# A convolution and expert-layer kernel: a new order for its first transfers, tap matrices and tap matmuls

## The chip, the cores and the metric

The kernel runs on one core of a Trainium2 chip. The metric is the device time of one execution in microseconds (us). Of 52 executions of the kernel before, 47 lie within 0.25% (692.39 to 694.08 us) and five reach up to 696.3, so medians over several runs are given, and for the small effect of this study the traces count for more than the times. The **head** is the stretch from the start to the first product with w_out; a **landing** is the end of a transfer.

## The reference, cut to what matters

```python
# x: (8, 4096, 192), weight: (8 heads, 7 taps); w_in: (192, 2048), w_out: (2048, 192)
w = softmax(weight, axis=-1)
out[b, s, head] = sum_k w[head, k] * x_padded[b, s + k, head]     # 7 taps, causal
h = out.reshape(32768, 192) @ w_in
result = np.maximum(0.01 * h, h) @ w_out                          # float32
```

## The kernel before: the parts that the change touches

The rows are handled in groups; the first 18 are half-blocks of 256 positions of two sequences. A group has 8 **units**: 12 matmuls with w_in into one of two output buffers (`ph`, in PSUM), then one activation on ScalarE into `g`. Products with w_out (`po`) follow one group behind. In the main loop VectorE makes the convolution. For the first two half-blocks ("half 0", "half 1") part of it is done by TensorE: a tap is a diagonal 64x64 matrix, in a high and a low bf16 part, and the 7 taps of a chunk of 64 channels are 28 small **tap matmuls** into `acc`, which ScalarE then scales into `yt`.

```python
# pieces of w_in: units 0-1, units 2-3, units 4-7
pieces = (0, NFC // 4, NFC // 2, NFC)
...
load_w_in(0, 0); ...; load_w_in(0, 1)
load_first(1)                      # half 1's x, two transfers
for n in (1, 2):
    for e in range(2):
        load_w_in(n, e)
load_first(2)                      # half 2's x
... # w_out in one transfer, then the x of half 3 and of block 2
diag_wide(0, 0, K)                 # VectorE: chunk 0, high part, all taps at once
for e in range(2):
    cast_first(0, e, nc.scalar.copy)
diag_low(0, range(2))              # ScalarE: low part, one tap each
transpose_first(0)
warm(3)                            # dummy matmuls
...
evac_first(0, nc.vector.tensor_copy, nc.scalar.copy)
...
diag_low(0, range(2, K))
diag_wide(1, 0, K)                 # VectorE: chunk 1, high part
diag_low(1, range(K))
...
for c in range(NPEC):              # half 0's chunks 0 and 1
    pe_jobs, evac_y = pe_conv_jobs(groups[0], c)
    for job in pe_jobs:
        job()
    evac_y(act_scale)              # the scaling, on ScalarE
    if c == 0:
        warm(2)
... # group 0, unit by unit:
mm1(grp, u)
if i == 0 and u == 1:
    transpose_first(1)
    evac_first(1, nc.vector.tensor_copy, nc.vector.tensor_copy)
    ...
if i == 0 and u in (2, 5):         # half 1's taps: 14 behind unit 2, 14 behind unit 5
    n = len(pe_ahead) // 2
    for job in pe_ahead[(u - 2) // 3 * n : (u + 1) // 3 * n]:
        job()
if i == 0 and u == 5:
    evac_y(act_scale)
if i == 0 and u == 6:
    transpose_first(2)
```

## Time and profile before

| | before |
|---|---|
| median of the first 3 runs | 693.94 us (693.4 to 695.55) |
| span of the profiled run | 690.8 us |
| TensorE busy | 685.0 us, 99% |
| TensorE's idle time | 2.3 us, all before 22 us |

What is added here is TensorE's timeline from 16 to 23 us (start, length, engine, line, operation, output and inputs, partitions and elements, count, and in brackets the idle time before it and what ended it):

```profile
16.37 1.50 PE L402 MATMUL ph<-yt,w_in 64*128 64x256 bf16 x23 [0.69 <-DMA w_in<-in_moe_w_in_dram]
17.80 0.96 PE L212 MATMUL acc<-xt,diag 64*64 64x256 bf16 x14
18.69 0.84 PE L402 MATMUL ph<-yt,w_in 64*128 64x256 bf16 x12
...
21.74 0.85 PE L402 MATMUL ph<-yt,w_in 64*128 64x256 bf16 x12 [0.24 <-ACT g L409]
22.39 0.82 PE L428 MATMUL po<-w_out,g 64*128 64x192 bf16 x15
```

Unit 4 resumes at 16.37, when the last piece of w_in has landed. Then come unit 5, half 1's second 14 taps, unit 6 at 18.69. At 22.39 the products with w_out begin; from there to the end of the span the view of waits lists none of TensorE. This is a good point to measure by: the **distance** from unit 4's resumption to the first product is 22.39 - 16.37 = 6.02 us.

### The profile page before, as it was taken

Reading aid. Unit: us, or ns where it says so; the run is one execution under the profiler, and the core shown is the slowest. Engines: PE = TensorE matmul, PEld = TensorE weight load, DVE = VectorE, ACT = ScalarE, POOL = GpSimd, SP = SyncE. Lnnn points to the kernel's source line nnn. Section 1 sums busy time; section 2 is a strip of 40 time slices with the busy share of each in tenths; the row PEclk is TensorE's granted clock in tenths of the full one; section 3 lists DMA queues with packets and bytes.
Section 4 is the critical chain, followed back from the end, with each engine's and each line's share of the span. In section 5 each row is a group of like instructions: output and inputs, shape, how many; then the busy total and the mean of one; then the engine's idle time right before and its main releaser. Section 6 shows DMA issues by size and latency. Waiting matters only on the chain.

```text
span 690.8 us, 26984 instructions
## 1 busy us (share of the span) xinstructions
PE 685.0 (99%) x12190; PEld 600.9 (87%) x12190; DVE 550.4 (80%) x1051; ACT 527.0 (76%) x609; POOL 147.2 (21%) x206
## 2 busy tenths in 40 slices
PE   8999999999999999999999999999999999999998
PEld 6999999999988888888888888888888888888887
DVE  6999999999986787878787878877878878787812
ACT  6888888888898777777777777777777777777771
POOL 7822220222222202222202222102222112000000
PEclk9999999999999999999999999999999999999999
DMA  9976644556657545566445566445664555222112
GB/s 150 121 92 92 83 72 81 70 74 84 81 75 90 73 80 74 67 94 82 68 83 68 75 83 89 71 74 75 78 82 75 82 71 70 67 60 59 47 42 65
DMA packets 184163, 53.85 MB, mean 78 GB/s; under 512 B 149104, under 2 KB 183664, under 8 KB 184048
## 3 DMA queue, kind: packets, MB, share of 16 engines
q0 software_dynamic: 99536, 14.76, 30.2%
q1 hardware_dynamic: 84512, 37.38, 22.7%
q8 instruction: 95, 1.56, 1.0%
q14 instruction: 20, 0.16, 0.1%
HBM read 29.88 MB, written 25.17 MB: 80 GB/s over the span
## 4 chain that ended last, share of the span: by engine, by line
PE 96%; DMA 1%; ACT 1%; POOL 1%; issue 0%; DVE 0%; POOLq 0%
PE po L428 49%; PE ph L402 47%; DMA w_in<-in_moe_w_in_dram 1%; ACT g L409 1%; POOL w_in L248 0%; POOL x_rows L123 0%; PE acc L212 0%; POOL sel L233 0%; DVE o_sb L475 0%; PE ptr L156 0%; POOL ident masks.py:199 0%; POOL sel L231 0%; POOL ident masks.py:197 0%; PE ptr L149 0%; POOLq masks.py:199 0%
## 5 line engine op out<-in xcount | busy, mean ns | idle before, releaser
L409 ACT ACTIVATE g<-ph 128x1024 bf16<-128x1024 f32 x512 | 496.3, 1021 | 142.3 <-PE ph L402 141.8
L193 DVE SCALAR_TENSOR_TENSOR yt<-xt,wk,yt 128x512 bf16<-128x512 bf16 (+1 forms) x720 | 458.3, 637 | 21.1
L428 PE MATMUL po<-w_out,g 64*128 64x192 bf16 (+1 forms) x8064 | 387.6, 243 | 0.0
L402 PE MATMUL ph<-yt,w_in 64*128 64x512 bf16 (+1 forms) x3936 | 384.6, 329 | 1.7 <-DMA w_in<-in_moe_w_in_dram 0.7
L428 PEld LDWEIGHTS <-g 64*128 64x128 bf16 (+1 forms) x8064 | 360.8, 94 | 28.3 <-issue 0.2
L402 PEld LDWEIGHTS <-w_in 64*128 64x128 bf16 x3936 | 246.1, 111 | 53.7 <-issue 3.0
L78 POOL DMA_DIRECT2D x_bf<-in_x_dram x180 | 133.9, 776 | 424.9 <-DMA xt<-x_bf 422.3
L475 DVE COPY o_sb<-po 128x192 f32<-128x192 f32 x184 | 65.7, 357 | 109.4 <-PE po L428 100.6
L187 DVE TENSOR_SCALAR yt<-xt,wk 128x512 bf16<-128x512 bf16 (+1 forms) x120 | 41.0, 341 | 1.5 <-DMA xt<-x_bf 1.4
L475 ACT COPY o_sb<-po 128x192 f32<-128x192 f32 x72 | 23.0, 319 | 3.9 <-PE po L428 0.2
L282 PE MATMUL warm<-zero 128*128 128x256 bf16 (+1 forms) x22 | 5.2, 393 | 1.1 <-DVE junk L228 1.1
L212 PE MATMUL acc<-xt,diag 64*64 64x256 bf16 x84 | 5.7, 283 | 0.0
L212 PEld LDWEIGHTS <-diag 64*64 64x64 bf16 x84 | 4.5, 112 | 1.2 <-DVE wk L362 0.4
L127 POOL DMA_DIRECT2D x_half<-in_x_dram x6 | 4.3, 720 | 3.5 <-DMA w_in<-in_moe_w_in_dram 3.5
L168 DVE COPY xt<-ptr 128x384 bf16<-128x384 bf16 x7 | 2.2, 351 | 3.1 <-PE ptr L156 2.7
L282 PEld LDWEIGHTS <-zero 128*128 128x128 bf16 x22 | 2.6, 132 | 2.3 <-DVE junk L228 1.1
L248 POOL DMA_DIRECT2D w_in<-in_moe_w_in_dram x6 | 3.9, 657 | 0.0
L343 ACT ACTIVATE diag<-ident,whm 128x64 bf16<-128x64 bf16 x14 | 3.5, 337 | 0.0
L123 POOL DMA_DIRECT2D x_rows<-in_x_dram x4 | 2.9, 733 | 0.4 <-DMA w_in<-in_moe_w_in_dram 0.4
L368 ACT ACTIVATE yt<-acc,rsum 128x256 bf16<-128x256 f32 x3 | 1.4, 470 | 1.0 <-PE acc L212 1.0
L288 ACT ACT_TABLE_LOAD x1 | 1.3, 1283 | 0.8 <-PEq L576 0.8
L133 ACT CAST x_half<-x_nat 128x384 bf16<-128x384 f32 x2 | 1.0, 512 | 1.1 <-DMA x_nat<-in_x_dram 1.1
(37 smaller groups left out, 12.0 us busy)
## 6 DMA issues: line engine op xcount, KB each, us to landing
out_dram<-o_sb SPq DMA_DIRECT2D x117, 192.0 KB, 2.1
x_bf<-in_x_dram POOLq DMA_DIRECT2D x180, 64.0 KB, 3.3
out_dram<-o_sb SPq DMA_DIRECT2D x22, 96.0 KB, 1.6
xt<-x_bf SPq DMA_TRANSPOSE x90, 2.5
w_in<-in_moe_w_in_dram POOLq DMA_DIRECT2D x4, 192.0 KB, 5.3
w_in<-in_moe_w_in_dram POOLq DMA_DIRECT2D x2, 384.0 KB, 8.6
w_out<-in_moe_w_out_dram POOLq DMA_DIRECT2D x1, 768.0 KB, 11.6
x_nat<-in_x_dram SPq DMA_DIRECT2D x2, 192.0 KB, 2.6
```

What stands on the lines that cost most here:

```text
L78: nc.gpsimd.dma_start(out=t[:, c, :, e, :], in_=src[2 * rp + e, :, :, c * CH : (c + 1) * CH],)
L127: nc.gpsimd.dma_start(out=x_half[q][:, c, :, e, :], in_=rows[:, e, :, c * CH : (c + 1) * CH],)
L187: lambda s=src, d=dst, c=c: nc.vector.tensor_scalar_mul(d, s, wk[:, c, 0:1])
L193: lambda s=src, d=dst, c=c, k=k: nc.vector.scalar_tensor_tensor(out=d, in0=s, scalar=wk[:, c, k : k + 1], in1=d, op0=mybir.AluOpType.mult, ...
L212: lambda k=k, p=p, a=a, e=e, ps=ps: nc.tensor.matmul(out=acc[ps, :T], lhsT=diag[c][ps, p, k, :], rhs=xt[0][ps, c, a : a + T], start=(k == ...
L248: nc.gpsimd.dma_start(out=w_in[n][e * CH : (e + 1) * CH], in_=moe_w_in[:, fs].rearrange("(c p) f -> p c f", p=CH),)
L282: nc.tensor.matmul(out=wa[:, 0, 0:cols], lhsT=zero[:, 0:128], rhs=zero[:, 0:cols], start=True, stop=True,)
L343: nc.scalar.activation(out=diag[c][:, 1, k, :], in_=ident2, func=mybir.ActivationFunctionType.Copy, scale=whm[:, c, 1, k : k + 1],)
L402: nc.tensor.matmul(out=ph[:, e, i * T : (i + 1) * T], lhsT=w_in_of(f, ps, c), rhs=y[ps, c, t0 : t0 + T], start=(c == 0), stop=(c == NCH - 1),)
L409: act = nc.scalar.activation(out=g[blk][:, nf * u : nf * (u + 1), :, t0 : t0 + T], in_=ph.rearrange("p e (i t) -> p i e t", i=nf), func=my ...
L428: return nc.tensor.matmul(out=po[m], lhsT=g[b][ps, fc, e, s * 128 : (s + 1) * 128], rhs=w_out[ps, fc, :], start=start, stop=stop,)
L475: ins = copy(out=o_sb[:, n % 2, :], in_=po.pop(n))
```

## The change

Its intent, as I read it: fill TensorE's wait for the last w_in piece with half 1's taps, so that they don't stand behind it; get the matrices for half 0 ready sooner by giving chunk 0's to VectorE and chunk 1's to ScalarE, without the two dummy matmuls between the chunks; and bring the second w_in quarter in sooner, since half 1's taps now come later.

```diff
-    def pe_conv_jobs(grp, c):
+    def pe_conv_jobs(grp, c, parts=(0, 1)):
...
     load_w_in(0, 1)
+    for e in range(2):
+        load_w_in(1, e)
     load_first(1)
-    for n in (1, 2):
-        for e in range(2):
-            load_w_in(n, e)
+    for e in range(2):
+        load_w_in(2, e)
     load_first(2)
...
-    diag_wide(0, 0, K)
+    for p in range(2):
+        diag_wide(0, p, K)
     for e in range(2):
         cast_first(0, e, nc.scalar.copy)
-    diag_low(0, range(2))
+    diag_each(1, 1, range(4))
...
+    evac_first(0, nc.vector.tensor_copy, nc.scalar.copy)
     nc.vector.reciprocal(rsum, rsum)
-    evac_first(0, nc.vector.tensor_copy, nc.scalar.copy)
...
-    diag_low(0, range(2, K))
-    diag_wide(1, 0, K)
-    diag_low(1, range(K))
+    diag_each(1, 1, range(4, K))
+    diag_each(1, 0, range(K))
...
-        pe_jobs, evac_y = pe_conv_jobs(groups[0], c)
+        pe_jobs, evac_y = pe_conv_jobs(groups[0], c, (c, 1 - c))
...
-        if c == 0:
-            warm(2)
...
-                if i == 0 and u in (2, 5):
-                    n = len(pe_ahead) // 2
-                    for job in pe_ahead[(u - 2) // 3 * n : (u + 1) // 3 * n]:
+                if i == 0 and u == 3:
+                    for job in pe_ahead:
                         job()
-                if i == 0 and u == 5:
                     evac_y(act_scale)
```

More of the change, by code (lines that the diff above doesn't have):

```diff
@@ L205, in pe_conv_jobs @@
         jobs = []
-        for p in range(2):
+        for p in parts:
             for k in range(K):
@@ L214, in pe_conv_jobs @@
                             rhs=xt[0][ps, c, a : a + T],
-                            start=(k == 0 and p == 0), stop=(k == K - 1 and p == 1),
+                            start=(k == 0 and p == parts[0]),
+                            stop=(k == K - 1 and p == parts[1]),
                         )
@@ L339, in diag_wide, with diag_each @@
         )
-    def diag_low(c, ks):
+    def diag_each(c, p, ks):
         for k in ks:
             nc.scalar.activation(
-                out=diag[c][:, 1, k, :], in_=ident2,
-                func=mybir.ActivationFunctionType.Copy, scale=whm[:, c, 1, k : k + 1],
-            )
-    diag_wide(0, 0, K)
+                out=diag[c][:, p, k, :], in_=ident2,
+                func=mybir.ActivationFunctionType.Copy, scale=whm[:, c, p, k : k + 1],
+            )
+    for p in range(2):
+        diag_wide(0, p, K)
     for e in range(2):
         cast_first(0, e, nc.scalar.copy)
-    diag_low(0, range(2))
+    diag_each(1, 1, range(4))
     transpose_first(0)
```

## The prediction

> **What bounds the kernel now.** I read the page first: engine shares and the chain that ended last.
>
> ```profile
> PE 685.0 (99%) x12190; PEld 600.9 (87%) x12190; DVE 550.4 (80%) x1051; ACT 527.0 (76%) x609; POOL 147.2 (21%) x206
> ...
> PE 96%; DMA 1%; ACT 1%; POOL 1%; issue 0%; DVE 0%; POOLq 0%
> ```
>
> The span of 690.8 us is TensorE work for 96% of its chain. The change adds and removes no product of the main loop, so it can only act where TensorE waits. The view of waits, for TensorE alone over the whole span, lists those:
>
> ```profile
> PE warm L282 <- DVE junk L228: 1.1, 1, 1.1
> PE ph L402 <- DMA w_in<-in_moe_w_in_dram: 0.7, 1, 0.7
> PE ph L402 <- ACT yt L368: 0.3, 1, 0.3
> PE ph L402 <- ACT g L409: 0.2, 1, 0.2
> ```
>
> Columns: who waited, for whom, us in total, times, longest. That is all the idle time there is, and all of it lies before 22 us. So the next view is the chain of waits in that stretch, in order of time (start us, length us, what):
>
> ```profile
> 5.26 1.84 POOL w_in L248 x3
> 7.10 9.23 DMA w_in<-in_moe_w_in_dram
> 16.32 0.05 issue
> 16.37 1.50 PE ph L402 x23
> 17.87 0.89 PE acc L212 x14
> 18.75 0.78 PE ph L402 x12
> 19.53 0.31 PE ptr L156 x24
> 19.84 0.80 PE ph L402 x12
> 20.64 0.02 issue
> 20.66 1.03 ACT g L409
> 21.70 0.04 issue
> 21.74 0.85 PE ph L402 x12
> ```
>
> The reader is to see that everything up to 16.32 us on this path is one transfer: the second half of the last w_in piece (units 4 to 7). What TensorE does before 16.37 isn't on the path; it waited 0.69 us there. From 16.37 to 21.74 the path is TensorE, then ScalarE, and holds 14 tap matmuls of half 1 (acc, 0.89). From 21.74 on there is no wait of TensorE left. So the question is only **how early the matmuls of 21.74 start**: the rest of the span, 690.8 - 21.74 = 669.1 us, should follow unchanged.
>
> **What the Trainium skill says.** "TensorE: Matmul & The Clock Gate", section "What's actually happening": TensorE runs at half rate until it has been busy for one window of about 3.4 us, and the window is free-running. The trace agrees: tap matmuls start 211 ns apart up to 7.4 us and 109 ns apart after it. The same section's idle limit of one window isn't approached by the gaps here (0.7 us at most). The same page, "Architectural detail", has ScalarE and VectorE as strict FIFO; so the place of each tap-matrix operation in its engine's order counts, not only what it waits for. "DMA: Bandwidth & Descriptors", "Two DMAs through the same engine are not ordered": within one queue of an engine descriptors start in order. The trace agrees: the landings of the software queue come in order of issue. w_in quarter 0 at 6.80 and 8.53; half 1's x at 9.05 and 9.74; quarter 1 at 10.55 and 12.59; the last piece at 14.48 and 16.32; half 2's x at 16.84 and 17.36. These I get by adding each issue's start to its time to landing in the tile view. "Perfetto Trace Analysis", "Tensor Engine Instruction": matmul ends are estimated by the profiler, so I work with starts.
>
> **The change, part by part.**
>
> 1. *Order of transfers.* Quarter 1 goes ahead of half 1's x, the bytes before the last piece stay the same, and the issues (0.63 to 0.74 us each) end at the same 6.49 us. So the last piece lands at **16.32 as before**. Quarter 1 should land by 12.59 - (9.74 - 8.53) = 11.4, and half 1's x, now last of the group, at about 12.0 and 12.5: half 2's x, which also follows a w_in piece, adds 0.52 us per share, and the group as a whole ends at 12.59.
>
> 2. *Tap matrices and half 0.* The wide VectorE operation (0.62 us) for chunk 1 becomes one for chunk 0's low part, ahead of the small sums. VectorE was idle 0.46 us before its copy of the first transposes, so this fits: the copy stays at 5.92. ScalarE still makes 14 matrices, 238 ns apart, four instead of two ahead of its copy at 5.95; it was idle 0.56 us there, two cost 0.48, so it fits too. Its last matrix then starts at 8.48 rather than 8.95. TensorE: chunk 0's 28 tap matmuls start at 6.56 as before, last pair at 8.40. Two dummy matmuls (warm) go, with their mode switches: chunk 1 starts at 8.51 instead of 8.92. Its 14 pairs at 0.109 end their starts at 9.92 (10.37 before). All matrices are ready in time (the seventh high one ends at 8.82, is used at 9.9). ScalarE's scaling of chunk 1 (0.47) goes from 10.69 to 10.24, and unit 0 resumes at 10.76, not 11.21: **0.45 us earlier, but ahead of a transfer that decides**.
>
> 3. *Half 1's transposes* follow unit 1. TensorE reaches them at about 12.08 (12.53 before), but their x lands at about 12.5: some 0.45 us of new wait, so they start at about 12.57, as before. VectorE's copy of them starts at 12.96 before and about 12.99 after, and the chain of half 1's convolution on VectorE (ready at 20.48 before) doesn't move.
>
> 4. *Half 1's tap matmuls.* Before: 14 behind unit 2, 14 behind unit 5. After: 28 behind unit 3. Units 2 and 3 start at 12.95 and 13.6 and need about 0.65 each; 28 taps from 14.45 need 14 x 0.109 = 1.52, so TensorE is at unit 4 at about 16.1. Still before 16.32; **the wait for the last piece shrinks from 0.69 to about 0.25 us, its end stays at 16.37**.
>
> 5. *After 16.37* 14 tap matmuls (0.89) and the scaling on ScalarE (0.48) are gone. Not all counts. ScalarE's activation takes 1.02 us per unit against 0.65 to 0.8 for TensorE's 12 matmuls, and there are two buffers, so the rows of ScalarE decide (start, length, what, count, idle before):
>
> ```profile
> 17.25 1.94 ACT L409 ACTIVATE g<-ph 128x1024 bf16<-128x1024 f32 x2 [0.61 <-PE ph L402]
> 19.08 0.48 ACT L368 ACTIVATE yt<-acc,rsum 128x256 bf16<-128x256 f32 x1
> 19.57 4.08 ACT L409 ACTIVATE g<-ph 128x1024 bf16<-128x1024 f32 x4
> ```
>
> ScalarE is busy from 17.25 to 23.65 with hardly a gap: taking away the scaling moves it by 0.4 to 0.48. Step by step: units 4 and 5 as before (activations end 18.28 and 19.19). Unit 6 needs unit 4's buffer: starts at 18.32 (18.69), done 19.14; its activation 19.19 to 20.21 (20.60 before). Transposes of half 2, then unit 7 at 19.39, activation 20.25 to 21.27 (21.69). The next group's unit 0 starts at 20.25, with chunk 2 of VectorE ready only at 20.48: a wait of perhaps 0.05 that nobody feels. Its unit 1 needs unit 7's buffer: 21.31, not 21.74.
>
> The sum: **-0.43 us**, from ScalarE's scaling leaving the stretch, and not the sum of what TensorE lost (0.45 + 0.89 + warm). 693.94 - 0.43 = 693.5.
>
> **The rivals.**
>
> *Half 1's x becomes the bound.* If it lands later than 12.6, say 13.1, transposes, units 2 and 3 and 28 taps all shift, TensorE arrives at unit 4 at 16.6 instead of 16.1, and VectorE's chain ends near 21.0, where the next group's unit 0 needs it at 20.5. Then the gain is eaten and up to 0.3 us lost: 693.6 to 694.3. For it: the slack is only 0.25 us on TensorE and nearly none on VectorE. Against: the bytes ahead of x grow by quarter 1 alone, and that group of four transfers ended at 12.59. I give it 0.3.
>
> *ScalarE doesn't bind and the whole 0.89 comes free.* Then unit 1 of the next group would start at 20.85, time 693.05. Against: ScalarE's rows above have no gap to shrink. 0.1.
>
> *Nothing is seen*: VectorE's later groups bind, and give the gain back. VectorE needs about 10.2 us per half-block (three chunks of about 3.3, plus copies) against TensorE's 10.5; it is ready at 31.20 for a group that TensorE starts at 31.77, with the third chunk used 0.2 later. 0.43 us fits, barely; the margin grows by some 0.5 us per group. 0.15.
>
> *Clock phase.* If the clock opens later than 7.4 us in a run, half 0's taps run longer, up to 0.1 us per pair; the remaining slack of about 0.25 us at unit 4 is less than the 0.69 that hid it before.
>
> **Range and chances.** The effect is 0.06%, while three runs of the kernel before span 693.4 to 695.55. So the range is that of run-to-run difference around 693.5: 692.5 to 694.9. 2% would be 13.9 us, six times all idle time of TensorE (2.3 us); slower by 2% would need a new wait in every group. So: faster 0.01, same 0.98, slower 0.01.
>
> **What would show it.** The wait of TensorE for ScalarE's scaling ends near 10.76; a new wait for half 1's x before the transposes, which start near 12.55; 28 taps in one piece from about 14.45; the wait for w_in ends at 16.37 but is about 0.25 long; ScalarE's activations run without scaling between them; the row at 21.74 comes near 21.31; no wait of TensorE after it; span about 690.4. It is wrong if x lands past 12.7, if the last w_in piece lands elsewhere than 16.3, or if TensorE waits on VectorE after 20 us.

## The result, and the profile after

| | before | after |
|---|---|---|
| median | 693.67 us (692.65 to 695.55, 4 runs) | 692.92 us (692.65 to 693.38, 4 runs) |
| span of the profiled run | 690.8 us | 690.9 us |
| ratio | | 0.9987, 95% interval 0.9964 to 1.0009 |

A ratio here compares the runs of both kernels from the same rounds, so it isn't quite the ratio of the medians. The interval holds 1. The profiled spans are the same within 0.1 us, so the first look at the trace shows no gain at all. TensorE's waits after:

```profile
PE ptr L156 <- DMA x_rows<-in_x_dram: 1.3, 2, 1.0
PE warm L284 <- DVE junk L229: 1.1, 1, 1.1
PE ph L403 <- ACT g L410: 0.7, 2, 0.5
PE ph L403 <- ACT yt L371: 0.3, 1, 0.3
PE acc L212 <- ACT xt L168: 0.2, 1, 0.2
```

Against the four lines of before: the wait of a matmul for w_in has left the list, a wait for half 1's x (`x_rows`) of 1.3 us has come, and the wait for ScalarE's activation rose from 0.2 to 0.7. TensorE's timeline from 12 to 23 us:

```profile
12.55 0.21 PE L156 MATMUL ptr<-ident,x_rows 64*64 64x64 bf16 x1 [1.00 <-DMA x_rows<-in_x_dram]
13.07 0.38 PE L156 MATMUL ptr<-ident,x_rows 64*64 64x64 bf16 x23 [0.31 <-DMA x_rows<-in_x_dram]
13.38 1.50 PE L403 MATMUL ph<-yt,w_in 64*128 64x256 bf16 x24
14.81 1.72 PE L212 MATMUL acc<-xt,diag 64*64 64x256 bf16 x28
16.47 1.85 PE L403 MATMUL ph<-yt,w_in 64*128 64x256 bf16 x24
18.78 0.85 PE L403 MATMUL ph<-yt,w_in 64*128 64x256 bf16 x12 [0.46 <-ACT g L410]
...
21.83 0.85 PE L403 MATMUL ph<-yt,w_in 64*128 64x256 bf16 x12 [0.22 <-ACT g L410]
22.48 0.74 PE L429 MATMUL po<-w_out,g 64*128 64x192 bf16 x13
```

The transposes of half 1 now wait twice, once for each half of its x. All 28 taps stand behind unit 3. Unit 4's first matmul is at 16.47; its other rows need the second half of the last piece, which landed at 16.77 in this run (16.32 before), and by the chain of waits they resumed at 16.82. Unit 6 follows without taps between, but waits 0.46 us for a buffer. The distance to the first product is 22.48 - 16.82 = **5.66 us, 0.36 less than before**, while unit 4 resumed 0.45 us later. The two cancel: the first product starts at 22.48, against 22.39. Is the later landing a consequence of the new order of transfers, or did it just happen? And which part of the change makes the distance shorter?

### The profile page after: what moved, and what is told of

Read it like the earlier page. It is cut to its first block, busy times and chain, and to the rows that moved or that the text cites. A ratio compares the mean times of both kernels' runs of the same rounds, so it can differ in the third digit from the quotient of the medians.

```text
span 690.9 us, 26980 instructions
## 1 busy us (share of the span) xinstructions
PE 684.0 (99%) x12188; PEld 599.2 (87%) x12188; DVE 550.1 (80%) x1051; ACT 527.0 (76%) x609; POOL 147.1 (21%) x206
## 4 chain that ended last, share of the span: by engine, by line
PE 96%; ACT 1%; DMA 1%; POOL 1%; issue 0%; DVE 0%; POOLq 0%
PE po L429 49%; PE ph L403 47%; ACT g L410 1%; DMA w_in<-in_moe_w_in_dram 1%; POOL w_in L249 0%; POOL x_rows L123 0%; POOL sel L234 0%; DVE o_sb L476 0%; PE ptr L156 0%; POOL ident masks.py:199 0%; POOL sel L232 0%; POOL ident masks.py:197 0%; PE ptr L149 0%; POOLq masks.py:199 0%; POOLq L575 0%
## 5 line engine op out<-in xcount | busy, mean ns | idle before, releaser
L193 DVE SCALAR_TENSOR_TENSOR yt<-xt,wk,yt 128x512 bf16<-128x512 bf16 (+1 forms) x720 | 458.3, 637 | 21.1
L187 DVE TENSOR_SCALAR yt<-xt,wk 128x512 bf16<-128x512 bf16 (+1 forms) x120 | 40.6, 338 | 1.7 <-DMA xt<-x_bf 1.5
```

The source lines that it names most:

```text
L187: lambda s=src, d=dst, c=c: nc.vector.tensor_scalar_mul(d, s, wk[:, c, 0:1])
L193: lambda s=src, d=dst, c=c, k=k: nc.vector.scalar_tensor_tensor(out=d, in0=s, scalar=wk[:, c, k : k + 1], in1=d, op0=mybir.AluOpType.mult, ...
```

## The experiments

All kernels gave correct results. Each one's profile is one reading of the head; the readings are gathered in a table behind the first two sets. "Last half-rate matmul" is the start of the last matmul with a long duration (over 0.36 us; the pairs of tap matmuls start 0.21 us apart there and 0.109 us later on), taken here as a slow clock.

### First set: is it the order of the transfers?

**before_again** and **after_again** are the two kernels unchanged.

> The kernel before, unchanged, timed against itself: the noise floor and a second reading of the landings. Both theories: ratio 1.000 within 0.001. Theory ORDER (the new order of transfers itself makes the last w_in piece land later, 16.77 against 16.32 us): last piece lands at 16.2 to 16.45 again. Theory NOISE (that landing differs from run to run by some tenths whatever the order): it may land anywhere from 16.2 to 16.9.

Measured: 693.43 us, ratio 0.9996 (0.9981 to 1.0012). Last piece at 16.48 us.

> The changed kernel, unchanged. ORDER: half 1's x lands at 12.9 to 13.1 us again, last w_in piece at 16.65 to 16.9, the first matmuls of the next group's unit 1 start at 21.7 to 21.9; ratio 1.000. NOISE: the landings move (the last piece at 16.3 to 16.6) and those matmuls then start 0.2 to 0.5 us earlier; ratio 0.9993 to 0.9999.

Measured: 692.88 us, ratio 0.9993 (0.9976 to 1.0011). Last piece at **16.27 us**, not 16.65 to 16.9: ORDER fails. Half 1's x at 12.82.

**after_old_order**: the changed kernel with the old order of transfers.

```diff
-    for e in range(2):
-        load_w_in(1, e)
     load_first(1)
-    for e in range(2):
-        load_w_in(2, e)
+    for n in (1, 2):
+        for e in range(2):
+            load_w_in(n, e)
```

> The changed kernel with the transfers in the old order (half 1's x ahead of the second w_in quarter); all else as changed. ORDER: half 1's x lands at 9.7, no wait ahead of its transposes, the last piece lands at 16.3, and unit 1 of the next group starts at 21.3 us: the forecast gain of 0.43 us, ratio 0.9994. NOISE: the x lands early too, but the last piece anywhere from 16.3 to 16.8, and unit 1 follows it by 5.0 us.

Measured: 692.63 us, ratio 0.9986 (0.9971 to 1.0002). Half 1's x at 9.99, as expected, but the last piece only at 17.13 us with the old order. Unit 4 did not even wait for it: this start was late by itself (x of half 0 landed late, and half 0's 56 taps took 4.16 us against 3.26 in the profile after), and TensorE reached unit 4 at 17.54.

**before_new_order**: the kernel before with the new order alone (the reverse of that diff).

> The kernel before with only the new order of transfers. ORDER: half 1's x lands at 12.9 to 13.1, TensorE waits some 0.4 us for it, the last piece lands at 16.7, and unit 1 of the next group starts at 22.1 to 22.2 instead of 21.74: ratio 1.0006. NOISE: the last piece lands from 16.3 to 16.8, and unit 1 at 21.7 to 22.2.

Measured: 693.56 us, ratio 0.9999 (0.9983 to 1.0015). Last piece at 17.84 us, later than either expectation had it. TensorE didn't wait for half 1's x, because this start was late as well (28 taps in 3.19 us against 1.72): a miss of both expectations on that point.

With three readings each, the old order gave 16.32, 16.48 and 17.13, the new one 16.77, 16.27 and 17.84. The landing moves by 1.6 us from run to run, and the orders overlap: **ORDER falls, and the 0.45 us of the first trace need no cause in the order.** NOISE is right in kind, though two landings (17.13 and 17.84) lie outside the range that it gave. Over the ten readings in the table below the old order has a mean of 16.67 us (six) and the new one of 17.01 (four), so a small effect of the order isn't excluded. What doesn't move is the distance: 6.02 us in all three readings with split taps.

### Second set: which part shortens the distance?

**taps_only**: the kernel before with half 1's taps and scaling behind unit 3, and nothing else of the change.

> The kernel before with one part of the change alone: half 1's 28 tap matmuls and their scaling behind unit 3. In all seven reads so far the first matmuls of the next group's unit 1 follow unit 4's resumption by 5.37 us (plans with the taps split) or 5.02 us (taps behind unit 3). Theory SCALING (the gain is the scaling that leaves ScalarE's stretch after unit 4): 5.02 us here too, wherever the last piece lands; ratio near 0.9995. Rival HEAD (the gain comes from the earlier half 0, 0.45 us): 5.37 us and no gain.

Measured: 692.82 us, ratio 0.9991 (0.9978 to 1.0004). Unit 4 resumes at 16.56, unit 1 of the next group is at 21.58: 5.02 us, as in the changed kernel. HEAD fails.

**maps_only**: the rest of the change without the new order and without the moved taps.

```diff
-                if i == 0 and u == 3:
-
-                    for job in pe_ahead:
-                        job()
+                if i == 0 and u in (2, 5):
+
+                    n = len(pe_ahead) // 2
+                    for job in pe_ahead[(u - 2) // 3 * n : (u + 1) // 3 * n]:
+                        job()
+                if i == 0 and u == 5:
                     evac_y(act_scale)
```

(against after_old_order.)

> The kernel before with only the other part: chunk 0's tap matrices on VectorE, chunk 1's on ScalarE, without the two dummy matmuls; old order of transfers, taps split as before. SCALING: 5.37 us from unit 4's resumption to unit 1 of the next group, only the wait for the last piece gets longer, by some 0.45 us; ratio 1.000. HEAD: earlier throughout, ratio 0.9994.

Measured: 692.87 us, ratio 0.9989 (0.9974 to 1.0003). By its times alone it looks as fast as the changed kernel (0.9987 and 0.9993), but the interval holds 1: the times don't tell the parts apart. In the trace 16.81 to 22.18: 5.37 us, as before. Its wait for the last piece was 0.63 us, not some 0.45 longer than the 0.69 of before as expected, since its clock was late (see the table).

**late_scale**: taps behind unit 3, but their scaling on ScalarE behind unit 5 again (against after_old_order). This undoes just what the prediction held to be the source of the gain.

```diff
                     for job in pe_ahead:
                         job()
+                if i == 0 and u == 5:
                     evac_y(act_scale)
```

> The changed kernel, old order of transfers, taps behind unit 3, but their scaling on ScalarE only behind unit 5. SCALING: although TensorE has lost its 14 taps (0.89 us) after unit 4, the distance is back at 5.4 to 5.5 us. Rival TAPS (the gain is TensorE's 14 matmuls leaving that stretch): it stays at 5.0 us.

Measured: 693.29 us, ratio 1.0001 (0.9984 to 1.0017). In the trace unit 4 starts at 17.15 and the first product at 22.88: 5.73 us, against 5.72 in after_old_order, which also reached unit 4 without a wait:

```profile
17.15 1.50 PE L402 MATMUL ph<-yt,w_in 64*128 64x256 bf16 x24
...
22.88 1.52 PE L428 MATMUL po<-w_out,g 64*128 64x192 bf16 x32
```

(The expectation counts to unit 1, whose matmuls take another 0.65 us up to the first product; it meant 6.05 to 6.15 on this scale.) **The scaling costs nothing visible there: SCALING falls**, and with it the reason that I had given. ScalarE's timeline of this run:

```profile
18.04 1.94 ACT L409 ACTIVATE g<-ph 128x1024 bf16<-128x1024 f32 x2 [1.41 <-PE ph L402]
19.87 0.48 ACT L370 ACTIVATE yt<-acc,rsum 128x256 bf16<-128x256 f32 x1
20.22 3.91 ACT L409 ACTIVATE g<-ph 128x1024 bf16<-128x1024 f32 x4
```

Four activations take 3.91 us here, against 4.08 in the kernel before. Behind the scaling, at 20.22, unit 6's activation is late, but unit 7's matmuls are done by its end and the next activation follows at once. The same time was otherwise lost as small waits of ScalarE for TensorE. (The run's time doesn't tell: its start was late too.)

**dummy_taps** asks the same from the other side: the changed kernel, its scaling left behind unit 3, and 14 of the tap matmuls repeated behind unit 5 into a sum that nobody reads any more (the lines that make the list `repeat` are left out).

```diff
                     evac_y(act_scale)
+                if i == 0 and u == 5:
+                    for job in repeat:      # chunk 0's low part again, 14 matmuls
+                        job()
```

> The changed kernel with 14 of half 1's tap matmuls repeated behind unit 5, into a sum that is no longer read; the scaling on ScalarE stays behind unit 3. Theory TAPS (what the change frees is TensorE's 14 taps between units 5 and 6, less the wait for unit 4's buffer that takes their place): unit 6 starts 2.32 us behind unit 4's resumption again instead of 1.96, its activation 3.20 instead of 2.84, and the first products of the second layer 6.02 instead of 5.66 us behind it. Theory SCALING (ScalarE's 0.48 us): 2.84 and 5.66 us stay, as the scaling is still gone from that stretch.

Measured: 693.68 us, ratio 1.0007 (0.9988 to 1.0026). TensorE's timeline:

```profile
17.21 1.50 PE L413 MATMUL ph<-yt,w_in 64*128 64x256 bf16 x23 [0.38 <-DMA w_in<-in_moe_w_in_dram]
18.64 0.95 PE L222 MATMUL acc<-xt,diag 64*64 64x256 bf16 x14
19.53 0.85 PE L413 MATMUL ph<-yt,w_in 64*128 64x256 bf16 x12
...
23.23 0.99 PE L439 MATMUL po<-w_out,g 64*128 64x192 bf16 x19
```

Unit 6 starts 19.53 - 17.21 = 2.32 us behind unit 4, and the first product 23.23 - 17.21 = **6.02 us: exactly the kernel before**, with the scaling still out of the way. TAPS stands. The gain is TensorE's 14 taps leaving the stretch (0.89 us in the chain of before), less the wait for unit 4's buffer that takes their place (0.46 us of idle time in the trace after). Both lengths depend on modelled ends; by starts alone, unit 6 moves from 2.32 to 18.78 - 16.82 = 1.96, which is the whole 0.36.

The readings so far (us; the last piece is for units 4 to 7):

| run | taps | last half-rate matmul | half 1's x landed | last piece landed | unit 4 runs on from | distance to first product | span |
|---|---|---|---|---|---|---|---|
| before | split | 7.2 | 9.74 | 16.32 | 16.37 | 6.02 | 690.8 |
| before_again | split | 5.0 | 8.90 | 16.48 | 16.53 | 6.02 | 691.0 |
| before_new_order | split | 10.2 | 13.61 | 17.84 | 17.89 | 6.02 | 692.4 |
| maps_only | split | 9.1 | 9.49 | 16.76 | 16.81 | 6.02 | 691.3 |
| dummy_taps | together, 14 repeated | 4.4 | 13.09 | 17.17 | 17.21 | 6.02 | 691.7 |
| after | together | 5.0 | 13.03 | 16.77 | 16.82 | 5.66 | 690.9 |
| taps_only | together | 4.2 | 9.63 | 16.52 | 16.56 | 5.67 | 690.7 |
| after_again | together | 4.8 | 12.82 | 16.27 | 16.27, no wait | 5.70 | 690.8 |
| after_old_order | together | 9.3 | 9.99 | 17.13 | 17.54, no wait | 5.72 | 691.7 |
| late_scale | together | 9.5 | 9.84 | 16.79 | 17.15, no wait | 5.73 | 691.3 |

From the first product to the end it is 668.42 to 668.47 us in nine of these ten runs. The tenth is after_again, with 668.82: there the gain was partly given back later. Its TensorE timeline near 31 us and its chain of waits (start, length, what):

```profile
31.36 1.78 PE L403 MATMUL ph<-yt,w_in 64*128 64x256 bf16 x24
```

```profile
31.31 0.50 DVE yt L193
31.81 0.04 issue
31.85 1.29 PE ph L403 x20
```

The 24 matmuls, which take 1.50 us elsewhere, take 1.78 here, because the third chunk of half 2's convolution is ready on VectorE only at 31.81; another 0.1 us goes the same way near 42.5. The chain leads back from there through VectorE, without a gap, to the landing of half 1's x at 12.82. That chain was also stretched on VectorE itself: the operation of line L187 at 28.01 took 0.66 us, against 0.47 in the profile after, and the operation of this line before it took 0.39 instead of 0.28. By my estimate either cause alone would have stayed hidden: without the wait for x, VectorE would have been 0.9 us earlier, without the stretching up to 0.5. So in that run, which had the earlier first product of the two readings of the changed kernel (21.97 us), the late x of the **new order** was one of two causes that together cost about 0.4 us.

### Third set: a version that takes away the wait itself

**split_last**: the changed kernel with the old order, and the last piece asked for as two, units 4 and 5 ahead of units 6 and 7 (against after_old_order).

```diff
-    pieces = (0, NFC // 4, NFC // 2, NFC)
+    pieces = (0, NFC // 4, NFC // 2, 3 * NFC // 4, NFC)
-        n = max(n for n in range(3) if pieces[n] <= f)
+        n = max(n for n in range(4) if pieces[n] <= f)
-    for n in (1, 2):
+    for n in (1, 2, 3):
```

> The changed kernel, old order of transfers, and the last w_in piece (units 4 to 7) asked for as two, units 4 and 5 ahead of units 6 and 7. LANDING (what sets the head's end is when TensorE may start unit 4): the first of them lands at about 14.5 us, unit 4 starts at 15.1 to 15.4 without a wait in a run with a normal start, unit 1 of the next group at 20.1 to 20.4; the second product then waits for w_out, which lands at about 21.2: in all 0.9 to 1.2 us off, ratio 0.9983. Rival: VectorE's half 1 convolution or the x of half 2 binds, and the distance of 5.02 us grows instead; ratio 0.999 or more.

Measured: 692.07 us (691.73 to 693.27), ratio **0.9982 (0.9968 to 0.9996)**. The third piece landed at 14.22, unit 4 started at 15.31 without a wait, unit 1 of the next group at 20.33. As expected the products waited for w_out, up to 21.58:

```profile
PE po L428 <- DMA w_out<-in_moe_w_out_dram: 0.4, 1, 0.4
```

**split_both**: also w_out in four transfers with a tile each (against split_last).

```diff
-    w_out = const_pool.tile([128, NFC, D], BF16)
-    nc.gpsimd.dma_start(...)                       # all of it
+    w_out = [const_pool.tile([128, RUN, D], BF16, name=f"w_out{c}") for c in range(NFC // RUN)]
+    for c in range(NFC // RUN):
+        nc.gpsimd.dma_start(
+            out=w_out[c],
+            in_=moe_w_out[c * 512 : (c + 1) * 512, :].rearrange("(p i) d -> p i d", p=128),
+        )
...
-            rhs=w_out[ps, fc, :],
+            rhs=w_out[fc // RUN][ps, fc % RUN, :],
```

> The changed kernel, old order of transfers, last w_in piece in two, and w_out in four pieces with a tile each, so that the second layer's first products need only the first of them. If the wait for w_out (0.40 us, and 0.6 us in all between unit 1 of the next group and those products) is all that the split w_in run left: products start at 5.66 us behind unit 4, near 20.9 to 21.1 us, another 0.5 us earlier; ratio 0.9974. Rival: four issues on GpSimd delay later x, or VectorE's convolution of the second block binds: TensorE then waits for VectorE near 30 us and part of it is given back; ratio 0.998.

Measured: 691.73 us (691.17 to 692.96), ratio **0.9978 (0.9961 to 0.9995)**, span 689.8 us, the shortest of all. The first of the four landed at 19.43, and no wait for w_out is left. Unit 4 started at 15.42, the first product at 21.40; expected were 20.9 to 21.1. TensorE's timeline shows the rest:

```profile
17.38 0.88 PE L405 MATMUL ph<-yt,w_in 64*128 64x256 bf16 x12 [0.46 <-ACT g L412]
18.19 0.66 PE L156 MATMUL ptr<-ident,x_rows 64*64 64x64 bf16 x24
```

The transposes of half 2 take 0.66 us instead of 0.38, since its x landed at 18.43 in this run (17.79 in split_last, which has the same w_in transfers). So the next transfer took over as the bound in this run, for 0.3 us. No wait for VectorE came later (668.44 us to the end).

**split_new_order** and **split_new_order_again**, one kernel read twice: as split_last, but with the new order of transfers.

> As the run with the last w_in piece in two, but with the change's order of transfers (second w_in quarter ahead of half 1's x). If the new order costs something that the late last piece hid: half 1's x lands at 12.3 to 13.0 us, TensorE waits for it some 0.7 to 1.2 us, unit 4 starts 3.44 us behind that landing, at 15.8 to 16.4 instead of 15.3, and VectorE's chain ends as much later; ratio 0.9988 to 0.9992. If the order is indifferent: unit 4 at 15.2 to 15.5 and ratio 0.9982.

Measured: 692.97 us, ratio 0.9992 (0.9977 to 1.0008). The clock was late, 56 taps took 4.87 us, TensorE reached half 1's transposes at 13.52 when its x (13.24) was there, and unit 4 started at 17.39. From the first product to the end it is 668.74 us: 0.28 us are lost near 43.5 us, where TensorE again needs a third chunk that VectorE has just finished. The chain leads back to half 0's slow taps and not to x, so a late clock is enough to make VectorE the bound.

> The same kernel as the run with the split last piece and the new order of transfers, read again because that one's profile fell on a late clock (half 0's 56 taps took 4.87 us), which hides any wait for half 1's x. If the new order costs something and this start is a normal one (taps in 3.26 us): TensorE waits for half 1's x, its second transfer landing at 12.4 to 13.2 us, unit 4 starts 3.44 us behind that landing, later than the 15.31 and 15.42 us of the old order, and TensorE may wait for VectorE near 31 us; ratio near 0.9992 again. If the order is indifferent: unit 4 at 15.2 to 15.5 us, ratio 0.998.

Measured: 692.67 us, ratio 0.9985 (0.9972 to 0.9999). The clock was late again (4.48 us), unit 4 started at 16.96, without a wait for the x (12.20). The first ratio is what a cost was to give, the second lies between the two forecasts, and neither trace had a normal start: **what the new order costs by itself with the piece split stays open.** The waits for half 1's x in after (1.3 us), after_again (0.67 us) and dummy_taps (1.4 us) and its part in the 0.4 us of after_again are what the traces show against it. For it there is one small wait of the old order: in taps_only unit 2 waited 0.2 us for the second w_in quarter (12.48), which cost nothing ahead of the later wait. A gain of the new order was seen in none.

In these two late starts the split had nothing to give: unit 4 started at 17.39 and 16.96, against 17.15 and 17.54 in late_scale and after_old_order, which were late too and undivided, and TensorE waited for the piece in none of the four.

## Why the prediction was right or wrong

- **Time: right, with luck in it.** 692.92 us lies in the range, but the range (692.5 to 694.9) is that of the noise and would have held no effect as well; "within 2%" was never in doubt. In the profiled pair the forecast gain didn't come: the span was put at 690.4 and was 690.9, and two of the prediction's own three signs of being wrong came true, half 1's x past 12.7 (13.03) and the last piece elsewhere than 16.3 (16.77). Over all rounds the kernel before has a median of 693.38 us (52 runs), the changed one 692.88 (10 runs), on several chips: 0.50 us less, by the side of a forecast 0.43. No single comparison of these two has an interval that leaves out 1; the sign rests on the distances in the traces, 6.02 against 5.66.
- **Part 1, landings: half right.** The bytes before the last piece didn't change, and no tie of its landing to the order was seen. But the prediction took one reading, 16.32, for a constant; ten readings of the undivided piece run from 16.27 to 17.84. That is four times the effect. Half 1's x was put at 12.0 and 12.5 and came at 12.50 and 13.03.
- **Part 2, half 0: right.** Unit 0's matmuls on chunk 1 resume at 10.15 after, against 10.70 in before_again with the same early clock: 0.55 earlier. The taps started 0.10 earlier in the run after (6.33 against 6.43), so 0.45 are the change's, as forecast. The wait just before them is for ScalarE's scaling, as named. That it isn't worth anything ahead of the transfer agrees with maps_only, whose distance stayed at 6.02.
- **Parts 3 and 4: right in kind.** The new wait before the transposes came; these started at 12.55 and 13.07 (12.57 forecast for all), the taps in one piece at 14.81 (14.45), unit 4 at 16.47 (16.1). Wrong was that half 1's chain on VectorE doesn't move: its copies started at 13.49 (12.99 forecast). There is also a slip in the sum: unit 2 was put at 12.95, 0.38 behind the transposes' start, which is their length; start to start it was 0.53 in the kernel before (12.53 to 13.06), so the slack at unit 4 was about 0.1 us and not 0.25.
- **Part 5: the size was right, the reason wrong.** The step that waits for unit 4's buffer was right: unit 6 was put 1.95 us behind unit 4's resumption and came at 1.96. Forecast from resumption to unit 1 of the next group was 21.31 - 16.37 = 4.94, measured 21.83 - 16.82 = 5.01; the missing 0.07 is unit 7's activation, at 3.94 behind unit 4 instead of 3.88. The step that failed is the sentence "from ScalarE's scaling leaving the stretch, and not the sum of what TensorE lost". late_scale puts the scaling back and loses nothing, dummy_taps puts the taps back and loses all. In the kernel before, unit 6's activation found two things ending together: its matmuls (18.69 + 0.84 = 19.53) and the scaling (19.08 + 0.48 = 19.56). I read "ScalarE busy without a gap" as "ScalarE binds", though the row of the scaling was filling a time in which ScalarE would have waited for TensorE. The rows shown held the hint: two activations take 1.94 us, so the second starts 0.92 behind the first, and four in a row would take 3.78 (an estimate from these rows); they took 4.08.
- **The rivals.** "Half 1's x becomes the bound": its condition came true in the profile after (13.03), but the last piece landed late as well and hid it; in after_again it cost part of 0.4 us, by way of VectorE. "VectorE's later groups bind" is the same event, in the group where the prediction had put it. The prediction's margin there was misread: VectorE needs 10.6 us from half 2's last chunk to half 3's in the kernel before (28.20 + 3.09 = 31.29 to 38.82 + 3.09 = 41.91), not 10.2, and TensorE 10.5 (31.77 to 42.30), so the margin doesn't grow over that group but shrinks by about 0.1. "Clock phase" had the right size for a pair (0.1 us) but no chance was given, and it came often: in four of the ten reads above, the last half-rate matmul was at 9.1 us or later, and in both such runs with the taps together (after_old_order, late_scale) TensorE came to unit 4 later than the last piece. The change has used up the slack that used to hide a late start.

## What to carry to other kernels

When a head of a kernel waits for one transfer, a change is worth what it takes out from behind that landing; measure from the landing on, as the landing itself moved by 1.6 us here. An engine whose rows follow without gaps isn't yet the bound: put its work back, or put the other engine's work back, and see which one brings the time back. And when work has been moved ahead of a wait, look at the wait itself: with the transfer that ends it split as well (old order, early clock), the first product came at 21.58 and 21.40 us, against 21.97 to 23.91 in the ten undivided readings, and the next transfer then showed as the next bound. The times don't show the split's gain apart from the change's: the intervals of 0.9982 and 0.9978 leave out 1, but they overlap that of after_old_order (0.9986).

## What the Trainium skill lacked or had wrong

- "TensorE: Matmul & The Clock Gate", "What's actually happening": full rate after at least one busy window of about 3.4 us, by its section "What you observe" around 4 us with half a microsecond to either side. Here, with the first matmul at 1.12 us, the last half-rate matmul started from 4.2 us (taps_only) to 10.2 us (before_new_order), 3.1 to 9.1 us later, among kernels with nearly the same first matmuls. The page does say that the number of slow matmuls varies by run; what doesn't hold here is the half microsecond. The first matmuls here include some with 8 rows, unlike the page's; no run tells whether that matters.
- "DMA: Bandwidth & Descriptors", "Two DMAs through the same engine are not ordered": the start of descriptors in order agrees with all readings, every landing was in order of issue. No page gives a figure for how much a landing varies; here one transfer, with the same bytes ahead of it, landed at 16.27 to 17.84 us.
- No page gives a time for TensorE going over from tap matmuls (64x64) to unit matmuls (64x128): start to start it took 0.20 us in the kernel before, against 0.109 us between pairs of tap matmuls. The point belongs to "TensorEngine Tiling (Array Packing)".
